# Soft-capped attention and gated convolution on one core: the middle words of the weights copied by GpSimd instead of fetched a second time, and every engine's order written anew

## The chip, the cores and the metric

The program runs on one core of a Trainium2 chip. The metric is the device time of one execution in microseconds (us), taken as the median of repeated runs. The engines are TensorE (PE: matmuls; its weight loads are shown apart as PEld), VectorE (DVE), ScalarE (ACT), GpSimd (POOL) and SyncE (SP, which issues all transfers here).

A measurement of this kernel tells a change from no change at about 0.5%, some 3.5 us.

## The reference

For 8 batches and 12 heads, 448 rows of 64, attention with a soft cap, then a gated feed-forward block on the joined heads (768 wide):

```python
scores = scale * np.matmul(q, k.transpose(0, 1, 3, 2))
scores = cap * np.tanh(scores / cap)
attn = np.exp(scores - max); attn = attn / (sum + 1e-09)
x = matmul(attn, v)                      # heads joined: (8, 448, 768)
gate = 1 / (1 + exp(-sum_k conv_w[k] * x shifted by k))     # 5 taps, per channel
out = (gate * (x @ w_val)) @ w_out
```

The weights `w_val`, `w_out` (768 x 768) and `conv_w` (5 x 768) arrive as 64-bit floats; everything else is float32.

## The kernel before

**Units of work.** Two heads make a pair, so there are 48 pairs, six to a batch; a batch is a block of the feed-forward part.

For a pair: q and k are loaded in 32-wide blocks (`load_blocks`, L335) and turned by DVE (`turn`, L457). PE makes the transposed scores in four chunks of 112 keys for both heads (`scores`, L478, PSUM tile `pss`, two buffers). ACT takes the tanh (L486) and the exp (L490) of each chunk (tile `pt`, 112 x 896).

PE then multiplies the chunk with V (`attnv`, L516, PSUM `psa`) and with ones for the row sums (`sums`, L532, `psz`). For later pairs DVE first adds chunks (`add`, L497 and L500, tile `pa`), so that fewer sums are needed.

DVE turns the sums, adds a guard, takes reciprocals (L538, L545, L546). POOL moves four small pieces of them across partitions (`shift`, L553 and L554, tile `rc`), DVE spreads them (L559) and multiplies (`mul`, L567), which frees `psa`.

From the result `u` follow a rounded copy by ACT (`x_hi`, L572), the rest by DVE (`x_lo`, L392), and five convolution steps (L584 on ACT, L588 on DVE).

From pair 13 on, q and k are also split into a rounded part and a rest (L463 on ACT, L392 on DVE), and a chunk of scores takes three passes in the rounded format, where it took plain float32 before.

For a block: `val` (L619, 3 pairs of column groups, each in four quarters) multiplies the six pairs' `xh`, `xl` with `wv`. The second and fourth quarter need the last three of the six pairs. DVE multiplies with the sigmoid (L594 on ACT; L647), ACT and DVE split the product (L650, L392), `out_part` (also L619) multiplies with `wo`, ACT copies the result out of PSUM (L678) and SP stores it (L682).

**Weights.** They are made in 12 steps of 256 rows by 384 columns. `weight_load` (L424) fetches the 64-bit numbers as pairs of 32-bit words into `w_raw` (one buffer). Of each number the split needs the upper word and a middle one: the upper 16 bits of the lower word next to the lower 16 bits of the upper one.

In the kernel before, `late_load` (L432) fetches the same 64-bit numbers again, shifted by two bytes in SBUF, into `w_late` (one buffer), so that each middle word lies on a word border and is read with a stride of two words.

Then `float64_split` works in three steps: ACT scales the upper word and overwrites it with its sign (L288, L289); DVE makes the high part (L292, L293); DVE masks the middle word and makes the low part (L297 to L299).

The five rows of `conv_w` go the same way, but there the middle words have always been copied by POOL (L320, 60 words of 16 bits).

**What sets the order.** Nothing is scheduled by a tool. The tables PAIRS, BLOCKS and WEIGHTS hold a number for each step, all steps are sorted by it, and each engine gets its instructions in that order. Each engine, SP's queue and POOL's too, works strictly in order. ACT's tanh and exp share a table, the sigmoid has another, and a change between them is an ACT_TABLE_LOAD.

Of the kernel before, what the change touches and what calls it, by code (L numbers as in the profile page):

```python
# [9 lines left out]
I32 = mybir.dt.int32  # L10
U16 = mybir.dt.uint16
# [35 lines left out]
- - -50.2578 -20.0082 -18.6802 - - - - -18.0026 -13.6506 -12.8893 -10.8337 -17.7336 -12.2984 -12.1683 -10.6814  # L47
  -15.7438 -11.0138 -9.0806 -8.4026 - - - -7.8583 -6.6164 -5.2762 -4.8421 -10.8956 -9.6536 -8.227 -6.5272 -6.4187
  -6.2991 -6.0315 -5.2231 -4.7395 -4.0222 -1.5948 -3.3443 -3.1754 -3.0638 -2.2435 -1.4958
-54.6543 -54.6682 -5.7398 -11.3558 -14.9308 - - - - -10.1607 -8.2226 -7.251 -8.8103 -8.766 -7.7723 -6.001 -7.503  # L50
  -7.9851 -7.0271 -5.5705 -7.2509 - - - -4.7942 -4.7791 -4.2203 -3.8644 -6.1487 -5.9805 -5.2522 -5.1652 -4.5697
  -4.2545 -4.0974 -3.8502 -2.9586 -2.9081 -1.1078 -2.6037 -2.0766 -1.4969 -1.2423 -0.7415
-8.5558 -10.828 -3.8585 -8.3819 -8.4517 - - - - -8.1909 -6.7346 -6.2205 -6.6099 -6.9986 -6.3265 -4.9873 -4.745 -6.5847
  -5.8479 -4.4232 -4.2656 - - - -3.5543 -3.3866 -3.1641 -3.0012 -5.1436 -4.2402 -4.2087 -3.8472 -3.7468 -3.4899
  -3.2181 -3.147 -2.6407 -1.157 -0.2141 -2.5015 -2.2091 -2.0732 -0.7817 -0.6342
-4.9902 -5.1452 -3.8143 -4.8984 -4.9319 - - - - -4.8453 -4.8201 -4.7117 -4.5313 -4.7619 -4.5375 -3.7333 -3.8994
  -4.0879 -4.4206 -3.5715 -3.6023 - - - -3.156 -2.3216 -2.1661 -2.1339 -4.0435 -3.5985 -3.5492 -3.322 -2.9828 -2.8443
  -2.611 -2.2872 -1.8844 -0.5716 -0.0119 -1.8513 -1.5372 -1.26 -1.1401 -0.8247
-5.1502 -5.5457 -3.7054 -4.6855 -5.0214 - - - - -4.5836 -4.0485 -4.49 -3.9663 -4.4152 -3.8796 -4.0604 -3.1655 -3.9467
  -3.4539 -3.3349 -3.0695 - - - -2.7667 -2.7181 -2.0325 -1.8895 -3.5521 -3.0355 -3.0189 -2.7694 -2.4562 -2.3389  # L60
  -2.3311 -2.007 -1.5129 -1.4622 -0.436 -1.2333 -0.8715 -0.7915 0.0531 0.3413
-4.7105 -4.9447 -3.6134 -4.1281 -4.1616 - - - - -3.9515 -3.871 -3.5726 -3.6641 -3.8144 -3.7573 -3.4104 -2.6706 -3.7204
  -3.2054 -2.8592 -2.6615 - - - -2.6022 -2.4665 -2.2458 -1.6562 -3.2862 -2.3588 -2.2561 -2.1821 -1.934 -1.9328 -1.728
  -1.6287 -1.5377 -1.4574 -1.2992 -0.1638 0.4232 1.0043 1.0532 1.7255
-3.992 -4.0342 -3.3279 -3.2028 -3.3106 - - - - -2.8324 -2.412 -2.4706 -3.0905 -2.7775 -2.1722 -2.3947 -2.9847 -1.8139
  -1.7614 -1.8089 -1.6615 -1.5463 -1.5365 - -1.8071 -1.3214 -1.0428 -0.828 -1.3963 -1.2032 - - -1.0303 -0.6544 -0.645
  -0.6132 -0.1329 2.0262 2.2951 -0.0875 0.1219 0.4106 1.5565 2.2947
-3.0587 -3.6384 -2.2123 -2.8324 -3.2508 - - - - -2.4022 -1.792 -2.1532 -1.1764 -2.1717 -1.144 -1.7627 -0.9081 -1.0652
  -0.7804 -1.1206 -0.4772 -0.327 -0.2744 - -0.3323 -0.2522 0.0203 0.0481 -0.2338 -0.1371 - - -0.0756 0.0724 0.2788
  0.5812 0.7204 2.5097 3.0808 0.9827 1.2949 2.7809 3.049 3.1704  # L70
# [837 lines left out]
```

## Time and profile before

| | |
|---|---|
| median of 3 runs | 704.95 us (704.92 to 708.12) |
| the profiled execution | 706.22 us, with a span of 704.4 us |
| PE busy | 679.7 us, 96% |
| ACT busy | 575.7 us, 82% |
| DVE busy | 556.7 us, 79% |
| POOL busy | 76.0 us, 11% |
| moved by DMA | 64.14 MB |

The span is what the trace covers, from the first instruction to the last; 1.8 us of the execution lie around it. The shares are means over the whole span, and the engines are not loaded alike in all of it: the weights are made, and the first two blocks' pairs are worked on, in the first 140 us. A count like x1248 is of matmul instructions in the trace, of which a few per cent can be missing.

### The profile page before, as it was taken

To read this page: it belongs to the slowest core of one execution; us is meant where nothing else is said; L and a number is where in the kernel's file an instruction comes from. 1 tells how busy PE (TensorE), PEld (TensorE's weight loads), DVE (VectorE), ACT (ScalarE), POOL (GpSimd) and SP (SyncE) were. 2 spreads that over 40 slices of the span, in tenths; PEclk is the share of its full clock that TensorE was granted. 3 is DMA by queue.
4 is the path that set the end of the run, shared out by engine and by line. 5 is a ranking of instruction groups with operands and counts; after the bars stand their busy time and mean duration, and the time that the engine had idled before them with its cause. 6 is when DMAs were issued, how large, how long until landed. Compare 5 with 4: busy or idle time off the path is not lost.

```text
span 704.4 us, 17118 instructions
## 1 busy us (share of the span) xinstructions
PE 679.7 (96%) x6896; PEld 492.6 (70%) x6896; DVE 556.7 (79%) x972; ACT 575.7 (82%) x738; POOL 76.0 (11%) x260
## 2 busy tenths in 40 slices
PE   5889999999999999999999999999999999999996
PEld 1323665577777787687677787767867878776996
DVE  1699999998897868988889776998897895896530
ACT  5999999988987797887996878878988887986121
POOL 0111100201010002110211100021000100011000
PEclk9999999999999999999999999999999999999999
DMA  6799999954414523243241332434323140211002
GB/s 134 167 190 235 181 213 231 240 122 83 78 32 95 102 41 67 62 92 60 49 80 50 78 72 44 75 77 105 60 53 69 45 111 8 60 38 46 1 3 93
DMA packets 241845, 64.14 MB, mean 91 GB/s; under 512 B 228448, under 2 KB 235616, under 8 KB 241760
## 3 DMA queue, kind: packets, MB, share of 16 engines
q1 hardware_dynamic: 241760, 62.98, 41.6%
q8 instruction: 56, 0.92, 0.6%
q14 instruction: 29, 0.24, 0.1%
HBM read 51.94 MB, written 11.01 MB: 89 GB/s over the span
## 4 chain that ended last, share of the span: by engine, by line
PE 66%; ACT 18%; DVE 6%; issue 3%; SPq 3%; DMA 2%; POOL 1%; ACTq 0%; DVEq 0%; POOLq 0%
PE psf L619 35%; PE psa L516 14%; PE pss L478 12%; ACT pt L486 5%; ACT pt L490 5%; PE pss L619 3%; ACT L490 2%; PE psz L532 2%; SPq L335 2%; ACT L594 1%; ACT g_h L650 1%; DVE pa L500 1%; DVE gate L588 1%; ACT gate L594 1%; POOL rc L553 1%
## 5 line engine op out<-in xcount | busy, mean ns | idle before, releaser
L486 ACT ACTIVATE pt<-pss,rc 112x896 f32<-112x896 f32 x192 | 189.3, 1003 | 42.9 <-PE psa L516 22.1
L490 ACT ACTIVATE pt<-pt,capt 112x896 f32<-112x896 f32 x192 | 194.6, 1041 | 0.9
L619 PE MATMUL psf<-wo,g_h 64*128 64x384 f32 x1248 | 165.0, 338 | 1.3 <-POOL token L627 1.3
L619 PE MATMUL psf<-xh,wv 64*128 64x448 f32 x1104 | 163.0, 369 | 0.2 <-ACT xh L572 0.2
L516 PE MATMUL psa<-pt,vn 112*32 112x448 f32 x1440 | 150.6, 542 | 0.7 <-DVE u L567 0.7
L619 PEld LDWEIGHTS psf<-wo,g_h 64*128 64x128 f32 x1248 | 116.6, 184 | 14.5 <-issue 4.7
L588 DVE SCALAR_TENSOR_TENSOR gate<-u,cw,gate 128x448 f32<-128x448 f32 x192 | 125.4, 664 | 1.4 <-ACT gate L584 0.4
L619 PEld LDWEIGHTS psf<-xh,wv 64*128 64x128 f32 x1104 | 106.5, 184 | 15.3 <-issue 3.8
L619 PE MATMUL psf<-wo,g_l 64*128 64x384 f32 x624 | 108.7, 332 | 0.0
L619 PE MATMUL psf<-xl,wv 64*128 64x448 f32 x552 | 103.8, 362 | 0.0
L500 DVE TENSOR_TENSOR pa<-pt 112x896 f32<-112x896 f32 x84 | 90.2, 1082 | 16.2 <-ACT pt L490 16.0
L516 PEld LDWEIGHTS psa<-pt,vn 112*32 112x32 f32 x1440 | 43.0, 109 | 71.4 <-issue 58.2
L478 PE MATMUL pss<-qt,kt 64*112 64x448 f32 x208 | 50.8, 586 | 13.0 <-DVE guard L401 7.8
L553 POOL COPY rc<-rc 32x7 f32<-32x7 f32 x96 | 32.0, 334 | 281.2 <-DVE rc L546 278.3
L619 PEld LDWEIGHTS psf<-wo,g_l 64*128 64x128 f32 x624 | 62.2, 184 | 0.0
L619 PEld LDWEIGHTS psf<-xl,wv 64*128 64x128 f32 x552 | 54.5, 184 | 3.7 <-DVE xl L392 0.4
L478 PE MATMUL pss<-qh,kh 64*112 64x448 f32 x280 | 54.6, 380 | 0.7 <-ACT pt L486 0.6
L478 PE MATMUL pss<-qh,kl 64*112 64x448 f32 x280 | 52.3, 363 | 0.3 <-DVE kl L392 0.3
L478 PE MATMUL pss<-ql,kh 64*112 64x448 f32 x280 | 52.2, 363 | 0.0
L678 ACT COPY osb<-psf 128x384 f32<-128x384 f32 x52 | 23.0, 481 | 35.0 <-PE psf L619 34.8
L559 DVE STREAM_TRANSPOSE zt<-rc 128x448 f32<-128x448 f32 x48 | 30.8, 641 | 25.8 <-POOL rc L554 25.3
L478 PEld LDWEIGHTS pss<-qt,kt 64*112 64x112 f32 x208 | 17.1, 178 | 36.1 <-ACT pt L486 13.4
(83 smaller groups left out, 812.2 us busy)
## 6 DMA issues: line engine op xcount, KB each, us to landing
vn<-in_v_dram SPq DMA_DIRECT2D x96, 112.0 KB, 2.8
out_dram<-osb SPq DMA_DIRECT2D x56, 192.0 KB, 2.1
kn<-in_k_dram SPq DMA_DIRECT2D x188, 56.0 KB, 2.4
qn<-in_q_dram SPq DMA_DIRECT2D x188, 56.0 KB, 2.5
w_raw<-in_moe_w_val_dram SPq DMA_DIRECT2D x12, 384.0 KB, 4.0
w_late<-in_moe_w_val_dram SPq DMA_DIRECT2D x12, 384.0 KB, 5.2
w_raw<-in_moe_w_out_dram SPq DMA_DIRECT2D x12, 384.0 KB, 3.8
w_late<-in_moe_w_out_dram SPq DMA_DIRECT2D x12, 384.0 KB, 5.5
```

The lines of the kernel that those rows point to most:

```text
L335: nc.sync.dma_start(t[g * BLK:(g + 1) * BLK].rearrange("p (c e) -> p c e", e=BLK), src[b, 2 * hp + j, :, d:d + BLK].rearrange("(c r) e -> ...
L478: nc.tensor.matmul(ps[:CH, j, :S], st[x][r, c], st[y][r], start=(n == 0), stop=(n == len(parts) - 1))
L486: nc.scalar.activation(st["p", i], st.pop(("s", i)), AF.Tanh, scale=rc8[:CH])
L490: nc.scalar.activation(t, t, AF.Exp, scale=capt[:CH])
L500: nc.vector.tensor_tensor(st["a", i], st["p", 2 * i], st["p", 2 * i + 1], op=ALU.add)
L516: nc.tensor.matmul(st["o"][r, :S], vloads[p][:, j, i, d:d + BLK], t[:, j], start=(i == 0), stop=(i == NKT - 1))
L532: nc.tensor.matmul(st["z"][r, :HQ], ones[:CH], t[:, j, q], start=(i == 0), stop=(i == n - 1))
L553: nc.gpsimd.tensor_copy(rc[GROUPS[g], 1], rc[GROUPS[g + 1], 1])
L559: nc.vector.transpose(st["zt"].rearrange("p (c e) -> p c e", e=BLK), rc)
L588: nc.vector.scalar_tensor_tensor(g, u[:, i:i + S], cw[:, hp, i:i + 1], g, ALU.mult, ALU.add)
L619: mm = nc.tensor.matmul(outs[k], left[r], right[r], start=(swap == 0 and first), stop=(swap == 1 and last))
L678: nc.scalar.copy(osb, psums.pop((b, "o", m))[:, :NH])
```

## The change

The second fetch is gone. In its place POOL copies the middle 16-bit words out of `w_raw` into a `w_late` of plain words (1536 of 16 bits for each partition), which DVE then reads without a stride:

```diff
-        def late_load(n):
-            w, c, nh, _ = wsteps[n]
-            late = wsc.tile([P, WC, 4 * NH + 2], U16, name="w_late", bufs=RB)
-            for i in range(WC):
-                r = (c.start + i) * P
-                nc.sync.dma_start(late[:, i, 1:1 + 4 * NH], w[r:r + P, nh * NH:(nh + 1) * NH].bitcast(U16))
-            wlate[n] = shifted(late, NH)
+        def low_words(n):
+            wlate[n] = wsc.tile([P, WC, NH], I32, name="w_late", bufs=RB)
+            nc.gpsimd.tensor_copy(wlate[n].bitcast(U16).rearrange("p i (n k) -> p i n k", k=2), wstate[n].bitcast(U16)[..., 1:3])
...
-            for f, when in zip((weight_load, late_load, weight_first, weight_second, weight_third), row):
+            for f, when in zip((weight_load, low_words, weight_first, weight_second, weight_third), row):
...
-CW_LOAD, CW_AT, W_FREE = -4.6636, -4.1717, 10.9638
+CW_LOAD, CW_AT, W_FREE = 2.1769, 2.7242, 10.5915
```

All three tables have new numbers; of WEIGHTS the first row, for instance:

```diff
--53.6683 -4.7397 -8.071 -6.4898 -4.4784
+0.4627 1.1297 1.297 1.3376 1.4463
```

The line numbers of the changed kernel are smaller by four behind the new function. No instruction is added or removed but the 24 fetches, the 12 copies and 6 ACT_TABLE_LOADs on the path that is taken (45 such loads between exp and sigmoid before, 51 now).

With its new place the copy must read `w_raw` before ACT's sign (L289) overwrites the upper word. It waits for the fetch and for the last read of the `w_late` before it (L299), and the next fetch into `w_raw` waits for the copy.

**DVE, the first weight step.** The rows after the turns of the second pair, before:

```order
L292 TENSOR_SCALAR w_t<-w_t 128x768
L293 TENSOR_TENSOR wv<-w_t,w_raw 128x2x384
L457 STREAM_TRANSPOSE kt<-kn 128x448
L538 STREAM_TRANSPOSE zt<-psz 128x224
L457 STREAM_TRANSPOSE qt<-qn 128x448
L545 TENSOR_SCALAR zt<-zt,guard 128x7
L546 RECIPROCAL rc<-zt 128x14
L559 STREAM_TRANSPOSE zt<-rc 128x448
L567 TENSOR_TENSOR u_63<-psa,zt 128x448
L297 TENSOR_SCALAR w_late<-w_late 128x2x384
L298 TENSOR_SCALAR w_t<-wv 128x768
L299 SCALAR_TENSOR_TENSOR wv<-w_late,w_t 128x2x384
```

The same place now (`u_63` is the result of the first pair):

```order
L292 TENSOR_SCALAR w_t<-w_t 128x768
L293 TENSOR_TENSOR wv<-w_t,w_raw 128x2x384
L297 TENSOR_SCALAR w_late<-w_late 128x768
L298 TENSOR_SCALAR w_t<-wv 128x768
L299 SCALAR_TENSOR_TENSOR wv<-w_late,w_t 128x2x384
L534 STREAM_TRANSPOSE zt<-psz 128x224
L453 STREAM_TRANSPOSE qt<-qn 128x448
L541 TENSOR_SCALAR zt<-zt,guard 128x7
L542 RECIPROCAL rc<-zt 128x14
L453 STREAM_TRANSPOSE kt<-kn 128x448
L555 STREAM_TRANSPOSE zt<-rc 128x448
L563 TENSOR_TENSOR u_63<-psa,zt 128x448
```

The low part of the first step has moved ahead of all of the first pair's division.

**ACT, the second weight step.** The rows from the middle of the third pair on, before (`cw` is the convolution's weights, `w_t` and `w_raw` a weight step, `xh` the rounded copy of a pair's result):

```order
L486 ACTIVATE pt<-pss,rc_110 112x896
L288 ACTIVATE cw_t<-cw_raw 128x30
L289 ACTIVATE cw_raw<-cw_raw 128x30
L572 CAST xh<-u_63 128x448
L490 ACTIVATE pt<-pt,capt 112x896
L584 ACTIVATE gate<-u_63,cw 128x448
L486 ACTIVATE pt<-pss,rc_110 112x896 x2
L490 ACTIVATE pt<-pt,capt 112x896 x2
L288 ACTIVATE w_t<-w_raw 128x768
L289 ACTIVATE w_raw<-w_raw 128x768
```

The same stretch now:

```order
L482 ACTIVATE pt<-pss,rc_110 112x896 x2
L288 ACTIVATE w_t<-w_raw 128x768
L289 ACTIVATE w_raw<-w_raw 128x768
L486 ACTIVATE pt<-pt,capt 112x896
L482 ACTIVATE pt<-pss,rc_110 112x896
L486 ACTIVATE pt<-pt,capt 112x896 x2
L482 ACTIVATE pt<-pss,rc_110 112x896
L288 ACTIVATE cw_t<-cw_raw 128x30
L289 ACTIVATE cw_raw<-cw_raw 128x30
```

The second weight step has moved ahead of the convolution's weights and of the first pair's rounded copy.

**POOL, around the first `val`.** Before, from the end of the sixth pair's division (`rc`) to the seventh's (`token` is a small write that orders two halves of a `val`):

```order
L553 COPY rc_768<-rc_768 32x7
L554 COPY rc_768<-rc_768 32x7
L627 MEMSET token_126 1x1
L553 COPY rc_987<-rc_987 32x7
L554 COPY rc_987<-rc_987 32x7
```

Now, between the same two divisions:

```order
L549 COPY rc_779<-rc_779 32x7
L550 COPY rc_779<-rc_779 32x7
L429 COPY w_late_790<-w_raw_756 128x1536
L623 MEMSET token_126 1x1
L429 COPY w_late_950<-w_raw_888 128x1536
L549 COPY rc_1018<-rc_1018 32x7
L550 COPY rc_1018<-rc_1018 32x7
```

Two of the copies stand in POOL's queue between the two divisions, one ahead of the token and one behind it.

More of the change, by code (lines that the diff above doesn't have):

```diff
@@ L185 @@
[L185 to L190 removed]
+- - 0.559 0.3888 0.6628 - - - - 0.8692 0.6629 1.2962 1.2963 1.1298 0.7229 1.2964 1.2968 1.2965 0.8691 1.2969 1.3452 -
+  - - 1.2967 1.3453 1.5034 1.7231 1.2966 1.2971 1.4464 1.4921 1.6292 1.7235 1.7237 1.9728 1.9729 3.3287 3.591 2.7562
+  2.9091 2.9093 3.0548 3.5031
@@ new lines @@
+-0.3373 -0.131 0.7233 0.1296 0.2961 - - - - 0.4465 0.4466 0.6291 0.568 0.4467 0.492 0.8942 0.6988 0.5681 0.629 0.9029
+  0.8943 - - - 1.0619 1.1767 1.2367 1.5081 0.6989 0.8941 0.985 1.04 1.0618 1.1768 1.3014 1.5077 1.7563 1.9689 1.969
+  1.909 1.9092 2.329 2.5036 3.0097
+-0.8701 -0.7185 0.5079 -0.2768 -0.2764 - - - - -0.097 -0.0969 0.3012 0.1097 -0.0273 0.0399 0.5076 0.3015 0.3679 0.3013
+  0.7243 0.4377 - - - 0.9089 0.997 1.0531 1.4329 0.45 0.7241 0.7561 0.9688 1.5029 1.5032 1.5033 1.5698 1.6311 2.6562
+  3.111 1.7067 2.1467 2.1473 2.1475 2.758
@@ new lines @@
+-1.106 -1.2766 0.433 -0.5622 -0.4511 - - - - -0.399 -0.2072 -0.3391 0.1177 -0.2756 0.1944 0.0532 0.2615 0.0547 0.3629
+  0.1246 0.4328 - - - 0.503 0.5035 0.6312 0.7928 0.3289 0.5204 0.6314 0.633 1.1466 1.1468 1.1472 1.1474 1.1476 2.0439
+  2.2003 1.2164 1.4943 1.7577 1.7579 2.1114
+-1.0029 -0.8822 -0.0574 -0.6712 -0.5669 - - - - -0.5668 -0.4972 -0.2704 -0.3304 -0.4974 -0.4303 0.0096 -0.0576 -0.3631
+  -0.1274 0.1465 0.0767 - - - -0.0139 0.3257 0.3929 0.4296 0.1469 0.2166 0.3927 0.3928 0.6907 0.7578 0.9648 1.1109
+  1.1111 1.2028 1.5126 1.4706 1.7485 1.9949 2.5694 2.697
@@ new lines @@
+-1.0575 -1.4966 -0.6744 -0.8529 -0.9232 - - - - -0.8523 -0.7416 -0.5059 -0.3092 -0.7417 -0.6745 -0.3095 -0.2424
+  -0.6074 -0.5058 -0.1752 -0.1054 - - - -0.2419 -0.1751 0.1108 0.2373 -0.3094 -0.1748 -0.0351 -0.0233 0.1112 0.1113
+  0.1358 0.2029 0.3043 0.4363 0.5802 0.5797 0.9948 1.0634 1.3801 2.9018
+-1.776 -1.7835 -1.1749 -1.1747 -1.7833 - - - - -0.7272 -1.1053 -0.9562 -1.0355 -0.4875 -1.0356 -0.7629 -0.8643 -0.3784
+  -0.8885 -0.1716 -0.2514 -0.005 0.0291 - 0.2396 0.2397 0.2399 0.24 0.2398 0.2403 - - 0.2824 0.3479 0.5696 0.614
+  0.7813 2.7576 2.8321 1.4998 1.5008 1.5487 2.5094 2.8722
@@ new lines @@
+-1.7628 -2.175 -0.3029 -1.4201 -1.5636 - - - - -1.4199 -1.3608 -0.5325 -0.7298 -1.2387 -0.6297 -0.3026 -0.4305 -0.3859
+  -0.2886 -0.2188 -0.3025 -0.2066 -0.1317 - 0.4992 0.4993 0.9017 0.9019 0.4995 0.4996 - - 0.5002 0.5933 1.1009 1.1682
+  1.1686 2.0419 2.0885 2.1287 2.3327 2.4188 2.5757 2.7089
+-2.7626 -2.7273 -0.4996 -2.293 -1.6935 - - - - -0.4999 -1.2185 -0.4991 -1.2186 -0.4997 -0.9236 -0.4927 -0.9907 -0.4994
+  -0.5009 -0.2648 -0.4066 -0.3745 0.1684 - 0.2163 0.2724 0.3285 0.3846 0.1687 0.1881 - - 0.5653 0.5656 0.5657 0.9168
+  1.042 1.3774 2.5913 1.2555 2.5914 2.6951 2.6954 3.0535
@@ new lines @@
+-2.3027 -3.3708 -0.0416 -1.4993 -2.3445 - - - - -1.0299 -1.098 -0.5508 -0.4909 -0.8992 -0.832 -0.4341 -0.2426 -0.5504
+  -0.3168 -0.1677 -0.1622 -0.2427 -0.0417 - 0.3329 0.333 0.3331 0.5756 0.1504 0.3328 - - 0.4634 0.6441 0.6445 0.7535
+  0.8038 1.2379 1.6832 1.2541 1.6829 1.6952 1.9012 2.0534
+-2.8409 -3.0249 -1.2425 -1.4346 -2.4928 - - - - -1.083 -1.3169 -0.8714 -0.9114 -1.0252 -1.0415 -0.5365 -0.5811 -0.534
+  -0.4641 -0.1558 -0.0811 -0.1561 0.3841 - -0.115 -0.0551 0.093 0.0931 0.1133 0.6828 - - 0.7314 0.9011 1.0408 1.1437
+  1.1941 1.3779 1.4061 1.378 1.975 2.0945 2.1479 2.4665
@@ new lines @@
+-2.4274 -2.899 -0.3047 -1.6227 -1.8715 - - - - -1.4876 -0.7623 -1.1559 -1.356 -1.156 -0.6722 -0.9067 -0.9843 0.0409
+  -0.616 -0.4091 -0.85 0.0533 0.0632 0.2756 0.3178 0.406 0.4621 0.5182 0.3778 - - - 0.4226 0.5183 0.5295 0.6325 0.6828
+  0.7335 0.8457 0.9154 0.9304 1.6011 2.4958 3.2074
+-2.8712 -3.1678 -0.1545 -2.0812 -1.7624 - - - - -1.2651 -0.959 -1.6723 -1.409 -0.2322 -0.3171 -1.5565 -1.2501 -0.1546
+  -0.0848 -1.479 -0.9589 0.0477 -0.4811 0.3539 0.2377 0.2976 0.3537 0.4099 0.466 - - - 0.5557 0.5558 0.6014 0.758
+  1.1868 1.4952 1.6562 1.5754 1.6116 1.887 2.2076 2.5684
@@ L237 @@
-2.5692 2.787 3.2505 3.6328 3.7017
-3.9699 4.8797 4.5859 4.8724 5.3787
-5.249 5.6583 5.9805 6.6296 6.6394
-6.7071 6.7617 7.0277 7.1294 7.2018
-7.2689 7.6346 7.8278 8.0635 8.0636
-8.1392 8.1665 8.529 8.8669 8.867
-9.3502 9.706 9.5098 9.869 9.8691
-10.2217 10.2728 10.4887 10.7188 10.7189
+0.4627 1.1297 1.297 1.3376 1.4463
+1.5035 1.973 2.177 2.2368 2.508
+2.5078 3.0533 3.0534 3.0549 3.5205
+3.5027 3.6313 3.7487 4.147 4.2238
+4.2239 4.4944 4.5323 4.9646 4.9647
+4.965 5.2002 5.3042 5.58 5.6217
+5.6218 6.0293 6.0633 6.2703 6.4676
@@ L245 @@
+6.3066 6.8684 6.8685 6.9432 7.0521
+7.0765 7.499 7.6256 7.7353 8.1685
+8.1681 8.4493 8.5092 8.5658 8.6833
+8.9169 9.0194 9.1289 9.1914 9.6444
+9.7536 9.8443 9.945 10.0158 10.0929
 """
-CW_LOAD, CW_AT, W_FREE = -4.6636, -4.1717, 10.9638
+CW_LOAD, CW_AT, W_FREE = 2.1769, 2.7242, 10.5915
 NPAIRED, NPLAIN = 11, 13
```

252 lines of the change are left out of this document (105 added, 147 removed), and 72 rows, old and new, of the table BLOCKS.

## The prediction

> **What bounds the kernel now.** I read the page first, then the table of stretches, then who PE and DVE wait for.
>
> ```profile
> span 704.4 us, 17118 instructions
> PE 679.7 (96%) x6896; PEld 492.6 (70%) x6896; DVE 556.7 (79%) x972; ACT 575.7 (82%) x738; POOL 76.0 (11%) x260
> ```
>
> PE is busy for 679.7 of 704.4 us, so 24.7 us are all that an order can win without taking work from PE. The change takes none: it has the same matmuls. The next table says where the idle time lies (each row: stretch, length, then the busy time of PE, PEld, DVE, ACT and POOL, the clock, the DMA share and GB/s).
>
> ```profile
> core 0: us, PE busy (x) PEld busy (x) DVE busy (x) ACT busy (x) POOL busy (x), PEclk, DMA share, GB/s
> 10.00:30.00 20.00, 17.33 (x130) 5.29 (x128) 7.95 (x15) 19.70 (x23) 0.97 (x5) 1.00 0.84 161
> 30.00:140.00 110.00, 105.73 (x974) 55.07 (x976) 102.70 (x183) 106.84 (x131) 17.45 (x42) 1.00 0.94 212
> 140.00:200.00 60.00, 59.96 (x608) 44.08 (x602) 53.63 (x93) 54.01 (x71) 5.19 (x21) 1.00 0.44 86
> 200.00:400.00 200.00, 198.34 (x2090) 152.36 (x2090) 168.93 (x293) 169.59 (x222) 24.55 (x78) 1.00 0.33 68
> 400.00:600.00 200.00, 198.56 (x2074) 151.91 (x2066) 163.96 (x284) 171.80 (x218) 18.96 (x74) 1.00 0.33 68
> 600.00:698.50 98.50, 97.62 (x1038) 82.81 (x1030) 57.63 (x101) 51.18 (x74) 8.49 (x33) 1.00 0.13 37
> 698.50:704.40 5.90, 0.00 (x0) 0.00 (x0) 0.00 (x0) 0.86 (x2) 0.00 (x0) 0.86 0.22 72
> ...
> ```
>
> Three parts are to be told apart. From 140 to 698.5 us PE alone is the bound: it idles for 558.5 - 554.5 = 4.0 us, while ACT and DVE are busy for four fifths of it (446.6 and 444.2 us). At the end 5.9 us go to the last copy and store. From 10 to 140 us three engines are full at once: PE idles for 130 - 123.1 = 6.9 us, ACT is busy for 126.5 of 130, DVE from 30 us on for 102.7 of 110, and the DMA engines for 0.94 of the time. All of the weights' work lies in this part, so it decides.
>
> ```profile
> PE pss L478 <- DVE guard L401: 7.8, 1, 7.8
> PE pss L478 <- ACT pt L486: 4.0, 8, 1.3
> ...
> ```
>
> Of PE's waits (total, times, longest) 7.8 us are the start, before the first scores, and what stands ahead of them on SP and DVE stays as it was. The next is for ACT's tanh, which frees the scores' PSUM tile. For a transfer PE does not wait. DVE's waits from 30 to 140 us begin so:
>
> ```profile
> DVE zt L559 <- POOL rc L554: 2.3, 6, 0.5
> ...
> DVE w_late L297 <- DMA w_late<-in_moe_w_out_dram: 0.5, 1, 0.5
> ```
>
> **The fetch that goes.**
>
> ```profile
> w_late<-in_moe_w_val_dram SPq DMA_DIRECT2D x12, 384.0 KB, 5.2
> w_late<-in_moe_w_out_dram SPq DMA_DIRECT2D x12, 384.0 KB, 5.5
> ```
>
> 24 transfers of 384 KB are 9.4 MB, out of the DMA's busiest time. What waited for them, though, is the 0.5 us above, on DVE. I take 0, with -0.5 as the other end: the load on the DMA engines falls, but nobody stands behind them.
>
> **ACT's and PE's order in the first part.** As ACT is full there, a PE step that needs an ACT result comes as late as the ACT work ahead of that result, and what matters is that sum against the PE work ahead of the step. I counted both in the two orders, up to the first `val` quarter of a block that needs the block's sixth `xh`. Prices:
>
> ```profile
> L486 ACT ACTIVATE pt<-pss,rc 112x896 f32<-112x896 f32 x192 | 189.3, 1003 | 42.9 <-PE psa L516 22.1
> L490 ACT ACTIVATE pt<-pt,capt 112x896 f32<-112x896 f32 x192 | 194.6, 1041 | 0.9
> L289 ACT ACTIVATE w_raw<-w_raw 128x768 f32<-128x768 f32 x12 | 11.2, 929 | 0.4
> L288 ACT ACTIVATE w_t<-w_raw 128x768 f32<-128x768 f32 x12 | 11.0, 914 | 0.0
> L584 ACT ACTIVATE gate<-u,cw 128x448 f32<-128x448 f32 x11 | 7.2, 658 | 0.0
> L594 ACT ACTIVATE gate<-gate 128x448 f32<-128x448 f32 x48 | 26.2, 573 | 2.3 <-DVE gate L588 2.0
> ```
>
> In block 0, ACT now has one tanh, one exp and one weight step more ahead of it, and one convolution step less: 1.00 + 1.04 + 1.84 - 0.66 = +3.2 us, while PE has only one chunk of scores more to do meanwhile. In block 1 it has two tanh less and one sigmoid more, -2.0 + 0.6 = -1.4 us, and PE one chunk of split scores less, three passes at 0.2 us (the pitch of L478 further below): -0.8 us net. So PE starts its first block later and has caught up by the second. Where PE falls furthest behind decides, and by the same count of the order before that was at block 1's place: I take -0.3 us, with -0.8 and +2.4 as ends.
>
> **PE's changes of format.** Counted in the order, PE goes from the rounded format to plain float32 and back 54 times before and 57 times now. One such excursion:
>
> ```profile
> 208.19 0.34 PE L619 MATMUL psf<-wo,g_l 64*128 64x384 f32 x2
> 208.46 0.96 PE L516 MATMUL psa<-pt,vn 112*32 112x448 f32 x8
> ...
> 211.98 0.46 PE L478 MATMUL pss<-qh,kh 64*112 64x448 f32 x2
> 212.28 0.36 PE L478 MATMUL pss<-ql,kh 64*112 64x448 f32 x2
> 212.48 0.37 PE L478 MATMUL pss<-qh,kl 64*112 64x448 f32 x2
> ```
>
> The way out costs about 0.1 us (0.27 where a pitch of 0.17 was due), the way back 0.1 us (0.30 in place of the 0.20 between the next two). Three more are +0.6 us.
>
> **ACT's table loads** rise from 45 to 51, at the price of this row:
>
> ```profile
> L490 ACT ACT_TABLE_LOAD x22 | 28.2, 1283 | 0.3
> ```
>
> That is 7.7 us of ACT. Up to block 1's place both orders have six changes of table, so the new ones lie behind it, where ACT waits for PE (of its 42.9 us ahead of tanh, 22.1 are for a matmul): 0. Without that cover it would be up to 7.7 us.
>
> **The copy on POOL.** Its form is in the trace once, with 60 words of 16 bits, as `cw_m`; around it stand a small copy that nothing disturbed, and a longer POOL instruction beside an idle DVE:
>
> ```profile
> L320 POOL COPY cw_m<-cw_raw 128x60 uint16<-128x60 uint16 x1 | 0.2, 234 | 1.5 <-DMA cw_raw<-in_moe_conv_w_dram 1.5
> 39.25 0.18 POOL L554 COPY rc<-rc 32x7 f32<-32x7 f32 x1
> 642.24 0.51 POOL L657 TENSOR_SCALAR g_h<-g_h 128x384 fp32r<-128x384 f32 x1
> ```
>
> From 7 to 60 elements the time rises by 0.05 us, from 7 to 384 by 0.33: about 0.9 ns for one. 1536 make 0.2 + 1.4 = 1.6 us, twelve times 19 us on an engine that has 17.45 of 110 us busy. The best case that the Trainium skill names (GPSIMD Engine Reference, section 3.1), 1.8 cycles for an element at 1.2 GHz, would make it an estimated 2.3 us; the rows here are faster.
>
> POOL's own time costs nothing. What it does to DVE may:
>
> ```profile
> 39.28 0.97 DVE L293 TENSOR_TENSOR wv<-w_t,w_raw 128x768 fp32r<-128x768 f32 x1
> 39.47 0.83 POOL L553 COPY rc<-rc 32x7 f32<-32x7 f32 x1
> ...
> 340.17 2.39 DVE L500 TENSOR_TENSOR pa<-pt 112x896 f32<-112x896 f32 x2
> 340.86 0.76 POOL L657 TENSOR_SCALAR g_h<-g_h 128x384 fp32r<-128x384 f32 x1
> 341.58 1.34 POOL L657 TENSOR_SCALAR g_l<-g_l 128x384 fp32r<-128x384 f32 x1
> 342.59 1.28 DVE L497 TENSOR_TENSOR pa<-pa,pa 112x896 f32<-112x896 f32 x1
> L500 DVE TENSOR_TENSOR pa<-pt 112x896 f32<-112x896 f32 x84 | 90.2, 1082 | 16.2 <-ACT pt L490 16.0
> ```
>
> A copy of 0.18 us took 0.83 because it came during a DVE instruction with two SBUF inputs, and ended with it. The other way round, two adds of 1.08 us took 2.39, 0.23 too long, and the next 0.2 too long, when POOL came between. So each holds the other up.
>
> The Trainium skill (SBUF — State Buffer, section "SBUF: two separate sides") has a rule for it: the two engines share one pair of ports as an exclusive lock, held for a whole instruction, and only DVE instructions in a two-port mode or with two SBUF inputs take part. By that rule alone a copy would stop such a DVE instruction for all of its 1.6 us; these rows agree in kind, at 0.2 us for an instruction of under half a microsecond.
>
> Two of the twelve copies come before 27 us, where DVE is mostly idle. For each of the other ten I bound DVE's loss by 0 (DVE is in its turns or in an instruction that reads PSUM) and 1.6 us (stopped for a whole copy). I take half, 0.8 us, since in the rows above POOL cost DVE 0.2 of its 0.4: 8 us. Against it stand 110 - 102.7 = 7.3 us of DVE idle time, of which some 5 can be used, and the low part of the first weight step, which now runs before the first pair's division:
>
> ```profile
> 27.53 0.57 DVE L297 TENSOR_SCALAR w_late<-w_late 128x768 int32<-128x768 int32 x1
> ...
> 28.60 0.96 DVE L299 SCALAR_TENSOR_TENSOR wv<-w_late,w_t 128x768 fp32r<-128x768 int32 x1
> ```
>
> From 27.53 to 29.56 that is 2.0 us out of the full part. 8 - 5 - 2 = +1.0 us, with 0 and 16 - 7 = +9 as ends. Behind a copy in POOL's queue stand the `rc` pieces for which DVE waits, and the `token` for which PE waits; behind ACT's sign (L289), which waits for the copy, stands all of ACT's work. The order puts the copies between two divisions, and ACT has the scaling (L288) to do ahead of the sign, so I take 0; if every copy began only as ACT came to its weight step, it would be 12 x (1.6 - 0.9) = 8 us.
>
> **The sum.** -0.3 + 0.6 + 0 + 1.0 = +1.3 us on a span of 704.4: 705.7, or 707.5 us with the 1.8 us around it. The profiled execution, 706.22 us, lies 1.3 us above the median of the runs, 704.95; from the median the forecast is **706.3 us**, no change that can be measured (0.5% is 3.5 us: 701.4 to 708.5).
>
> **Rivals.**
>
> *Slower: DVE becomes the bound of the first part.* If the copies stop DVE for their whole length, it loses 16 us there and can absorb 7: +9, and with the +0.3 of the other terms 714 us. It decides from (3.2 + 7) / 10 = 1.0 us of loss for one copy. For it: the 0.83 us row, and a DVE that already leaves only 7%. Against it: about a third of DVE's instructions there are turns or read PSUM. Signs that wait for their copies, above, would add to it. The time would be that of the lock in the Trainium skill (SBUF — State Buffer, "SBUF: two separate sides"), held at its fullest; the rows here show the lock, and none shows how long a copy of this size holds it. Chance 0.33.
>
> *Faster: the new order closes gaps.* The 6.9 us of PE idle time from 10 to 140 us and the 4.0 us behind it are what it could win; half of it is 5.5 us, which gives 699.5 us. For it: the DMA engines go from 0.94 to about two thirds, so loads come early, and all steps were free to move. Against it: ACT is busy for 126.5 of 130 us, and the same ACT work stands ahead of block 1. Chance 0.20.
>
> *That the second fetch stays, or the copies wait for it,* can't be: the order has no such row.
>
> **How the numbers follow.** No change has 0.47, slower 0.33, faster 0.20, each with a spread of some 3 us around its time. The range is 700 to 714 us: it leaves out a tenth at either end, and its upper end is the full stop of DVE. Within the no-change case alone it is 702 to 708.5.
>
> **What would show it.** In the profile after, POOL should have twelve copies of about 1.6 us (a mean up to 2.5, as they wait for DVE), the DMA share from 30 to 140 us about 0.65, DVE's busy time there some 5 us higher, and PE's idle time from 10 to 140 us within 3 us of 6.9. The first block's `val` should start some 2 us later than before, and the second block's where it was. The forecast is wrong if PE idles for 10 us or more there behind DVE, or for under 3; if the copies take over 3 us; or if PE's idle time behind 140 us leaves 4.0 by more than 2 us.

## The result and the profile after

| | before | after |
|---|---|---|
| median, first comparison (4 runs each) | 704.93 us | 713.38 us (712.28 to 714.16) |
| ratio | | 1.0108, 95% interval 1.0076 to 1.0140 |
| repeated beside other kernels (11 runs before, 5 after) | 707.06 us | 712.53 us, ratio 1.0080 (1.0067 to 1.0094) |

The change made the kernel slower by 0.8 to 1.1%. The range on record, 700 to 714 us, holds the time, though only just. The likeliest case, no change, was wrong, and so were two steps of its sum. Everything below is given as a ratio to the kernel before, run on the same chip in the same group; 1% is 7.1 us.

The page of the kernel after: span, then busy time and share of each engine.

```profile
span 712.0 us, 17107 instructions
PE 680.6 (96%) x6896; PEld 491.8 (69%) x6896; DVE 565.5 (79%) x972; ACT 583.7 (82%) x744; POOL 103.7 (15%) x272
```

PE's own work is the same (679.7 us before). DVE executes the same 972 instructions, but they take 8.8 us longer. The stretches of the kernel after (stretch, length, busy time of PE, PEld, DVE, ACT, POOL, clock, DMA share, GB/s):

```profile
30.00:140.00 110.00, 100.99 (x915) 53.82 (x909) 103.50 (x174) 102.15 (x127) 30.29 (x48) 0.98 0.63 131
...
10.00:140.00 130.00, 119.16 (x1063) 60.31 (x1061) 112.72 (x192) 121.92 (x148) 35.07 (x57) 0.99 0.66 131
140.00:698.00 558.00, 549.64 (x5728) 421.36 (x5726) 450.94 (x773) 457.46 (x589) 68.14 (x208) 1.00 0.30 63
```

The DMA share from 30 to 140 us fell from 0.94 to 0.63, as announced. But PE idles from 10 to 140 us for 10.8 us, where it was 6.9, and from 140 to 698 us for 8.4 us, where it was 4.0. So about 4 us were lost in each of two parts, and they have to be explained apart. PE's waits behind 140 us in the kernel after (total, times, longest):

```profile
PE psf L615 <- POOL token L623: 4.3, 4, 1.5
PE pss L474 <- ACT pt L482: 1.5, 2, 0.8
PE pss L474 <- DVE ql L392: 1.1, 2, 0.9
PE psa L512 <- DVE u L563: 0.9, 2, 0.6
PE psz L528 <- DVE pa L493: 0.7, 2, 0.4
```

These are 8.5 us. The same list of the kernel before adds up to 3.8 us, and begins so:

```profile
PE psf L619 <- POOL token L627: 1.3, 2, 1.0
PE psa L516 <- DVE u L567: 0.7, 2, 0.4
```

No copy begins behind 140 us, so this loss looks like one of the order. The copies themselves, in the kernel after (durations in ns: shortest, median, longest; then the first and the last start):

```profile
L429 POOL COPY w_late<-w_raw x12: 1464/1466/2118, 10.9 to 139.5; 128x1536 uint16<-128x1536 uint16 x12
```

What one of them does is seen at 115 us, in the timeline of the kernel after (start, duration, then in brackets the idle time before and who ended it):

```profile
114.98 0.62 DVE L563 TENSOR_TENSOR u<-psa,zt 128x448 f32<-128x448 f32 x1
115.38 1.46 POOL L429 COPY w_late<-w_raw 128x1536 uint16<-128x1536 uint16 x1 [3.90 <-DMA w_raw<-in_moe_w_out_dram]
115.51 1.81 DVE L392 TENSOR_TENSOR g_l<-gate,g_h 128x448 fp32r<-128x448 f32 x1
...
117.24 1.14 DVE L643 TENSOR_TENSOR gate<-psf,gate 128x448 f32<-128x448 f32 x2
117.89 0.56 ACT L646 CAST g_h<-gate 128x448 fp32r<-128x448 f32 x1 [3.71 <-DVE gate L643]
...
119.76 0.58 DVE L392 TENSOR_TENSOR g_l<-gate,g_h 128x448 fp32r<-128x448 f32 x1
...
124.00 1.01 PE L474 MATMUL pss<-qt,kt 64*112 64x448 f32 x4 [1.87 <-ACT pt L482]
```

The subtraction `g_l` takes 0.58 us at 119.76 and 1.81 us at 115.51, where the copy came with it. It ends at 117.32, about half a us behind the copy's end at 116.84, as if most of its work had begun only then. The product `gate` behind it on DVE is late by that, and ACT ends a wait of 3.7 us only then. PE still has work at that time; it pays at 124.00, where it waits 1.87 us for ACT. In the same order without copies (a kernel of the next section) ACT's wait is 1.14 us and PE's 0.42:

```profile
111.78 0.57 ACT L648 CAST g_h<-gate 128x448 fp32r<-128x448 f32 x1 [1.14 <-DVE gate L645]
...
117.87 1.01 PE L476 MATMUL pss<-qt,kt 64*112 64x448 f32 x4 [0.42 <-ACT pt L484]
```

Read in this way, ten copies lengthened DVE's instructions by 0 to 1.3 us each, 7.3 us in all.

### The profile page after: what moved, and what is told of

Read it like the earlier page. It is cut to its first block, busy times and chain, and to the rows that moved or that the text cites. A ratio compares the mean times of both kernels' runs of the same rounds, so it can differ in the third digit from the quotient of the medians.

```text
span 712.0 us, 17107 instructions
## 1 busy us (share of the span) xinstructions
PE 680.6 (96%) x6896; PEld 491.8 (69%) x6896; DVE 565.5 (79%) x972; ACT 583.7 (82%) x744; POOL 103.7 (15%) x272
## 4 chain that ended last, share of the span: by engine, by line
PE 58%; ACT 12%; DVE 11%; issue 2%; POOL 1%; DMA 1%; SPq 1%; ACTq 0%; DVEq 0%; POOLq 0%
PE psf L615 32%; PE psa L512 12%; PE pss L474 9%; ACT pt L486 4%; ACT pt L482 3%; PE pss L615 3%; ACT L486 2%; PE psz L528 2%; DVE gate L584 2%; DVE pa L496 2%; ACT g_h L646 1%; DVE pa L493 1%; DVE gate L643 1%; POOL rc L549 1%; DVE zt L555 1%
## 5 line engine op out<-in xcount | busy, mean ns | idle before, releaser
L496 DVE TENSOR_TENSOR pa<-pt 112x896 f32<-112x896 f32 x84 | 92.0, 1103 | 22.9 <-ACT pt L486 22.5
L549 POOL COPY rc<-rc 32x7 f32<-32x7 f32 x96 | 36.2, 378 | 283.7 <-DVE rc L542 281.2
L474 PE MATMUL pss<-qt,kt 64*112 64x448 f32 x208 | 52.3, 597 | 13.0 <-DVE guard L401 7.9
L646 ACT CAST g_h<-gate 128x448 fp32r<-128x448 f32 x48 | 26.4, 561 | 32.6 <-DVE gate L643 32.6
L643 DVE TENSOR_TENSOR gate<-psf,gate 128x448 f32<-128x448 f32 x46 | 27.3, 613 | 26.8 <-PE psf L615 26.8
```

The lines of the kernel that those rows point to most:

```text
L474: nc.tensor.matmul(ps[:CH, j, :S], st[x][r, c], st[y][r], start=(n == 0), stop=(n == len(parts) - 1))
L496: nc.vector.tensor_tensor(st["a", i], st["p", 2 * i], st["p", 2 * i + 1], op=ALU.add)
L549: nc.gpsimd.tensor_copy(rc[GROUPS[g], 1], rc[GROUPS[g + 1], 1])
L643: nc.vector.tensor_tensor(g, psums.pop((b, d))[:, :S], g, op=ALU.mult)
L646: nc.scalar.copy(gated["h"][:, d, TL:], gates[b * NPAIR + d])
```

## The experiments

**Theory A**: the copies stop DVE, and in a part where DVE has no time to spare the end is late by about as much. **Theory B**: the order written anew is what costs. A third question came up on the way: what the second fetch was worth.

| kernel | median | ratio to before | interval |
|---|---|---|---|
| old order, no fetch, no copy | 705.05 us | 0.9973 | 0.9960 to 0.9986 |
| old order, copies | 712.44 us | 1.0080 | 1.0066 to 1.0094 |
| old order, copies in four pieces | 707.96 us | 1.0015 | 1.0001 to 1.0030 |
| old order, SBUF-to-SBUF transfers | 734.77 us | 1.0394 | 1.0367 to 1.0420 |
| new order, no fetch, no copy | 707.16 us | 1.0005 | 0.9996 to 1.0014 |
| new order, copies (the change, repeated) | 712.53 us | 1.0080 | 1.0067 to 1.0094 |
| new order, copies in four pieces | 709.83 us | 1.0045 | 1.0031 to 1.0059 |
| new order, copies in eight pieces | 711.51 us | 1.0062 | 1.0044 to 1.0081 |
| new order, each copy twice | 722.36 us | 1.0215 | 1.0202 to 1.0229 |
| new order, spare copies later | 710.68 us | 1.0050 | 1.0036 to 1.0064 |
| new order, second fetch | 722.65 us | 1.0225 | 1.0206 to 1.0244 |
| new order, second fetch issued later | 717.74 us | 1.0146 | 1.0124 to 1.0168 |

### The change taken apart

**The order alone**: the new tables, with `late_load` in place of the copy, issued together with the first fetch.

```diff
-            for f, when in zip((weight_load, low_words, weight_first, weight_second, weight_third), row):
-                at(when, f, n)
+            for f, when in zip((weight_load, late_load, weight_first, weight_second, weight_third), row):
+                at(row[0] if f is late_load else when, f, n)
```

> The new order alone: every step stands where the changed kernel has it, but the middle parts are fetched a second time, as before, and GpSimd copies nothing. Theory A (the copies' hold on VectorE costs the first part its 5 to 6 us, the order only some 3 us behind it, less 2 us at the end): 706 to 708 us, PE idle from 10 to 140 us near 7 us. Theory B (the new order itself makes the kernel slower): 711 to 714 us, PE idle from 10 to 140 us still near 11 us. In both, PE's waits for the token on POOL stay as in the changed kernel if they belong to the order.

Measured 1.0225, outside of both. PE's waits in this kernel:

```profile
PE pss L478 <- DVE guard L401: 7.8, 1, 7.8
PE psa L516 <- DMA vn<-in_v_dram: 6.8, 4, 2.4
PE psf L619 <- POOL token L627: 4.3, 4, 1.5
PE psf L516 <- DMA vn<-in_v_dram: 3.4, 2, 2.2
```

And those of SP's queue from 10 to 145 us (L432 is the second fetch):

```profile
SPq L432 <- DVE wv L299: 10.9, 5, 3.8
SPq L432 <- DVE wo L299: 8.1, 4, 3.1
```

PE now waits 10.2 us for `vn`, for which it never waited in the kernel before: the second fetch waits 19 us in SP's queue for its buffer, with the loads of q, k and v behind it. So this run can't judge between A and B; it shows that the new order does not go with a second fetch at this place. The waits for the token are those of the kernel after (4.3 us), so they do belong to the order.

**The copy alone**: the old tables and `low_words` as in the change, at a place between the landing and the scaling.

```diff
+                if f is low_words:
+                    when = row[2] - 0.0001 if n == 0 else (max(row[0], done) + row[2]) / 2
```

> The copy alone: the order of before, the second fetch gone, and each GpSimd copy placed midway between the landing of its weights (and the end of the weight step ahead) and its scaling on ScalarE. Theory A: ten copies stop VectorE for about 0.7 us each, of which the 7 us of idle time take a part; 708 to 712 us, and PE's idle time behind 140 us stays near 4 us. Theory B: 704 to 706 us.

Measured 1.0080, 5.7 us, as A has it (712.44 us is 0.4 above A's range, but the kernel before is 1.8 us slower in this group than the 704.95 us that the range was reckoned from). Behind 140 us PE idles for 4.4 us, near the 4.0 of the kernel before, as A said too.

**The new order without fetch and copy**; `lates[0]` is one tile, set to 1.0 once, so this kernel leaves out the middle words of the weights:

```diff
-            nc.gpsimd.tensor_copy(wlate[n].bitcast(U16).rearrange("p i (n k) -> p i n k", k=2), wstate[n].bitcast(U16)[..., 1:3])
+            wlate[n] = lates[0]
```

> The changed kernel without its copies and without a second fetch: the low parts are computed from one constant tile, so the low halves of the weights are wrong, and VectorE, ScalarE and TensorE have the same instructions in the same order as in the changed kernel. Theory A: 706 to 708 us, with VectorE's busy time from 30 to 140 us some 6 us lower. Theory B: 712 to 714 us. Beside the run with the order alone it shows what the second fetch costs in this order: both within 1 us if it costs nothing.

Measured 1.0005: A's value. Its page and its two stretches:

```profile
PE 678.5 (96%) x6896; PEld 490.7 (69%) x6896; DVE 558.2 (79%) x972; ACT 583.3 (82%) x744; POOL 83.7 (12%) x261
```

```profile
10.00:140.00 130.00, 123.31 (x1120) 63.14 (x1118) 111.45 (x201) 127.52 (x156) 15.61 (x45) 0.99 0.72 137
140.00:698.00 558.00, 549.55 (x5742) 423.54 (x5741) 444.93 (x764) 452.99 (x585) 67.02 (x208) 1.00 0.30 63
```

Without the copies PE idles 6.7 us in the first part, as before the change. Behind 140 us it still idles 8.5 us (8.4 with the copies), so that loss is the order's and not the copies'. DVE's busy time over the whole span is 7.3 us lower than with the copies, as read off one by one above. From 30 to 140 us it is only 1.5 us lower (102.05 against 103.50), where 6 were expected; that sign missed.

**The kernel before without its second fetch**, the same edit in the old order, and **the change again**, beside it:

> The kernel before in its old order, without the second fetch and without any copy: the low parts come from one constant tile, so the low halves of the weights are wrong. If the fetch cost nothing in the old order: the time of before within 1 us. If the DMA's load of 0.94 did hold something up: 1 to 5 us faster. Against the kernel without copies in the new order (equal to before) it says which of the two orders is the better one once neither has a fetch or a copy: the same if the orders are worth the same, 2 us or more faster if the new order loses what I read in its trace behind 140 us.

> The changed kernel again, unaltered, beside the others of this group. Its ratio to the kernel before should come out near the first one, 1.0108; what the kernel without copies (ratio 1.0005) lies below it is the price of the copies in the new order.

Measured 0.9973 and 1.0080. With these the corners can be subtracted. They come from two groups on two chips, each set against its own runs of the kernel before; by the intervals in the table each difference holds to 1 to 1.5 us:

- The fetch that goes: 0.9973 - 1 = -0.27%, -1.9 us.
- The order, with neither fetch nor copy: 1.0005 - 0.9973 = +0.32%, +2.3 us.
- The copies in the new order: 1.0080 - 1.0005 = +0.75%, +5.3 us; in the old order 1.0080 - 0.9973 = +1.07%, +7.6 us.

The timelines say where the copies' price is paid. PE's first `val` matmul of block 1 and its last matmul, in the new order without copies and then with them:

```profile
158.02 0.67 PE L617 MATMUL psf<-xh,wv 64*128 64x448 f32 x4
...
700.95 0.34 PE L617 MATMUL psf<-wo,g_l 64*128 64x384 f32 x2
```

```profile
162.76 0.68 PE L615 MATMUL psf<-xh,wv 64*128 64x448 f32 x4
...
705.97 0.34 PE L615 MATMUL psf<-wo,g_l 64*128 64x384 f32 x2
```

And the old order without copies and with them:

```profile
159.07 0.58 PE L617 MATMUL psf<-xh,wv 64*128 64x448 f32 x4
...
696.91 0.34 PE L617 MATMUL psf<-wo,g_l 64*128 64x384 f32 x2
```

```profile
166.30 0.58 PE L615 MATMUL psf<-xh,wv 64*128 64x448 f32 x4
...
704.08 0.34 PE L615 MATMUL psf<-wo,g_l 64*128 64x384 f32 x2
```

In the new order PE is 4.7 us late at block 1 and 5.0 us at the end, in the old one 7.2 us at both places. All of the price is paid before block 1, and PE wins back nothing of it later, where it idles for only 4 to 9 of 558 us. The spans of the first pair differ by less, 707.4 and 710.8 us: from the start of the last matmul to the end it took 6.4 us in one execution and 4.8 in the other.

The clock is a rival that the rows can answer. In the old order the granted clock is 1.00 from 30 to 140 us with copies and without, and there they cost most. In the new order it is 0.98 in both traces. Of the five runs of the change repeated, the one with a mean clock of 1.0 took 711.96 us and the four at 0.995 to 0.997 took 712.25 to 713.43, while nine of the eleven without copies had 0.999 or 1.0; so an estimated half a us of the 5.3 may be the clock's.

### Is it DVE that the copies stop?

**Each copy twice**, one behind the other:

```diff
             nc.gpsimd.tensor_copy(wlate[n].bitcast(U16).rearrange("p i (n k) -> p i n k", k=2), wstate[n].bitcast(U16)[..., 1:3])
+            nc.gpsimd.tensor_copy(wlate[n].bitcast(U16).rearrange("p i (n k) -> p i n k", k=2), wstate[n].bitcast(U16)[..., 1:3])
```

> The changed kernel with each GpSimd copy done twice, one behind the other. Theory A: VectorE has no idle time left to absorb a second copy, so ten more copies at 0.7 to 1.5 us each add 7 to 15 us: 720 to 728 us. Theory B: under 2 us more, 713 to 715 us.

Measured 1.0215, 9.5 us above the single copy: A. Its page:

```profile
PE 682.5 (95%) x6896; PEld 491.4 (68%) x6896; DVE 573.7 (80%) x972; ACT 583.5 (81%) x744; POOL 127.0 (18%) x284
```

The second copies lengthened DVE's work by 8.2 us (573.7 against 565.5). ACT's signs wait for a copy for 6.4 us there, 0.3 with the single copy, so not all of the 9.5 us need be DVE's.

**Four pieces**, of one row block and half its columns each:

```diff
-            nc.gpsimd.tensor_copy(wlate[n].bitcast(U16).rearrange("p i (n k) -> p i n k", k=2), wstate[n].bitcast(U16)[..., 1:3])
+            o, i = wlate[n].bitcast(U16).rearrange("p i (n k) -> p i n k", k=2), wstate[n].bitcast(U16)[..., 1:3]
+            for j in range(WC):
+                for h in range(2):
+                    r = slice(h * NPH * P // 2, (h + 1) * NPH * P // 2)
+                    nc.gpsimd.tensor_copy(o[:, j, r], i[:, j, r])
```

> The changed kernel with each copy cut into four pieces of 384 elements (0.4 us each by the measured 1.47 us for 1536). If VectorE loses time because one GpSimd instruction holds the port until it ends, a piece can stop it for 0.4 us at most and the two take turns: 709 to 712 us, with VectorE's instructions stretched by under 0.5 us each. If the loss goes with the words copied and not with the length of one instruction: 713 to 714 us, as the changed kernel.

Measured 1.0045, 709.83 us, the first of the two, with the copies' price cut from 0.75 to 0.40%. The mechanism shows in one small instruction, the mask of the convolution's weights (L298 on 30 words), in the kernels without copies, with whole ones, with four pieces and with eight:

```profile
35.46 0.18 DVE L298 TENSOR_SCALAR cw_t<-cw 128x30 int32<-128x30 int32 x1
```

```profile
35.80 1.47 POOL L429 COPY w_late<-w_raw 128x1536 uint16<-128x1536 uint16 x1 [3.41 <-DMA w_raw<-in_moe_w_val_dram]
...
35.89 1.42 DVE L298 TENSOR_SCALAR cw_t<-cw 128x30 int32<-128x30 int32 x1
```

```profile
35.92 0.96 POOL L433 COPY w_late<-w_raw 128x384 uint16<-128x384 uint16 x2 [0.69 <-DMA w_raw<-in_moe_w_val_dram]
...
36.01 0.46 DVE L298 TENSOR_SCALAR cw_t<-cw 128x30 int32<-128x30 int32 x1
```

```profile
34.43 2.57 POOL L433 COPY w_late<-w_raw 128x192 uint16<-128x192 uint16 x8 [2.17 <-DMA w_raw<-in_moe_w_val_dram]
...
35.83 0.33 DVE L298 TENSOR_SCALAR cw_t<-cw 128x30 int32<-128x30 int32 x1
```

0.18 us of work take 1.42, 0.46 or 0.33 us, following the length of one GpSimd instruction (medians of 1.47, 0.51 and 0.35). The Trainium skill (SBUF — State Buffer, section "SBUF: two separate sides") describes a pair of ports that GpSimd and a DVE instruction take as an exclusive lock for a whole instruction, and these rows agree with it: DVE's instruction ends just behind the end of one on POOL (37.31 and 37.27 us with whole copies).

**Eight pieces** (`range(4)` and quarters of the columns in the code above):

> The changed kernel with each copy in eight pieces of 192 elements. By the lock held for one instruction, a piece stops VectorE for some 0.3 us at most: ratio between 1.001 and 1.004 (four pieces gave 1.0045, no copies 1.0005), if GpSimd's longer total time (some 33 us of copies instead of 18) makes no sign wait. If the loss only follows the number of collisions: 1.0045 or more.

Measured 1.0062, no better than four; by the medians it is worse, but the intervals overlap. By its size this is the second branch, but the condition of the first did not hold either: cut this small, the twelve copies take POOL longer in all (96 x 0.352 = 33.8 us by the median of a piece), and signs do wait. ACT's waits from 10 to 140 us:

```profile
ACT pt L486 <- PE pss L478: 3.8, 1, 3.8
ACT w_raw L289 <- POOL w_late L433: 3.1, 4, 0.9
```

With four pieces the signs wait 0.7 us in all. DVE also waits 5.9 us for a load of q with eight. Whether either of the two ate up the gain is not shown; cutting finer than four brought nothing more.

**Spare copies later**: the new order without copies, and twelve that nobody needs between 204 and 584 us (1408 elements each).

```diff
+        for n in range(12):
+            at(15.5 + 2.5 * n, spare_copy, n % 4)
```

> The kernel without copies (new order, low halves wrong), with twelve copies that nobody needs put between about 240 and 640 us, one every 35 us or so, each of 1408 elements in the same form. VectorE is busy there for 84% and TensorE is the bound. If a copy costs only where VectorE has no time to spare: within 1.5 us of the kernel without copies, so a ratio of 0.999 to 1.003. If a copy costs its 0.5 us wherever it stands: 712 to 714 us, ratio near 1.009.

Measured 1.0050, between the two expectations. The page and the two stretches:

```profile
PE 678.7 (96%) x6896; PEld 490.5 (69%) x6896; DVE 566.5 (80%) x972; ACT 583.1 (82%) x744; POOL 103.6 (15%) x273
```

```profile
10.00:140.00 130.00, 122.41 (x1114) 61.88 (x1112) 112.11 (x200) 127.27 (x155) 16.80 (x45) 1.00 0.72 137
140.00:698.00 558.00, 549.17 (x5732) 423.24 (x5730) 452.57 (x765) 453.24 (x586) 85.64 (x219) 1.00 0.30 62
```

Here too DVE's work grows by 8.3 us (566.5 against 558.2). In the stretch with the copies PE's busy time is only 0.4 us smaller (549.17 against 549.55), but a fixed stretch does not hold the same work in both. So the two matmuls from above are the better measure, here in the kernel with the spare copies:

```profile
158.72 0.68 PE L622 MATMUL psf<-xh,wv 64*128 64x448 f32 x4
...
702.87 0.34 PE L622 MATMUL psf<-wo,g_l 64*128 64x384 f32 x2
```

At block 1 PE is 0.7 us later than without copies (158.02), at the end 1.9 (700.95). The first 0.7 us stand ahead of every spare copy; they may come from the edit's other side (the constant tile lies elsewhere and is read in another way), which was not tested. The copies cost PE the other 1.2 us, a seventh of what DVE lost, where in the first part 5.3 of 7.3 us were lost. So where PE alone is the bound most of it is hidden, and not all. The timed difference, 0.45% or 3.2 us, is larger than these 1.9. Most of the rest is that the profiled execution without copies, 709.25 us, lay 2.1 us above its median, and the one with the spare copies 0.6; the clock of the former fell to 0.91 from 30 to 50 us, where the other's stayed at 1.00.

### What could take the copy's place

**The second fetch issued later**, behind the end of the weight step that frees its buffer:

```diff
-                at(row[0] if f is late_load else when, f, n)
+                at(max(row[0], done + 0.0001) if f is late_load else when, f, n)
```

> The new order with the second fetch (no copy), but each second fetch issued only behind the end of the weight step ahead, which frees its buffer, and no longer together with the first fetch. If the 15 us of the run with the order alone come from SP's queue, where the loads of q, k and v stand behind a fetch that waits for its buffer: 707 to 711 us (ratio 1.001 to 1.006), and PE waits for vn no longer. If they come from the bytes themselves (DMA share): still 718 us or more.

Measured 1.0146, a third of the way back and next to the second expectation. Over the first 160 us the queue's waits of these two kinds at L432 fell only from 23.0 to 19.9 us, so SP comes to the fetch early all the same, and the waits for `vn` to 6.9 us. That the place in the queue is a part of the price is shown; how much the bytes themselves cost in this order is not settled.

**A transfer from SBUF to SBUF**, in the old order:

```diff
-            nc.gpsimd.tensor_copy(wlate[n].bitcast(U16).rearrange("p i (n k) -> p i n k", k=2), wstate[n].bitcast(U16)[..., 1:3])
+            nc.gpsimd.dma_start(late[:, :, 1:1 + 4 * NH], wstate[n].bitcast(U16).rearrange("p i n k -> p i (n k)"))
```

> A version meant to beat both: the old order, the weights fetched once, and the middle parts made by a transfer from SBUF to SBUF (the raw words again, shifted by 16 bits) issued from GpSimd's queue as soon as the buffer is free, in place of the copy. The old order with neither fetch nor copy has ratio 0.9973. If the transfers land before ScalarE comes to its sign: 0.997 to 1.000, and VectorE's busy time as in that kernel (556 us). If the signs wait for the landing, 1 to 2 us for each of twelve: 1.015 to 1.03.

Measured 1.0394, by the second branch and beyond it. Its transfers (KB and median us from issue to landing) and ACT's and SP's waits from 10 to 140 us:

```profile
w_late<-w_raw POOLq DMA_DIRECT2D x12, 768.0 KB, 5.3
```

```profile
ACT w_raw L289 <- DMA w_late<-w_raw: 19.8, 8, 4.3
...
SPq L424 <- DMA w_late<-w_raw: 32.3, 9, 5.1
```

Eight signs wait 19.8 us in all, and the next fetch into the one `w_raw` waits too, with the loads behind it.

**Four pieces in the old order**, the two edits above together:

> The old order with the copy in four pieces (as the copy alone, 1.0080, but each copy cut into four of 384 elements). Without fetch and copy the old order has 0.9973, so whole copies cost 1.07% there. If the pieces' gain belongs to the port and not to the order, they save here what they saved in the new order, 0.35% or somewhat more: ratio 1.002 to 1.005. If what they gained in the new order was a matter of that order's places: 1.007 to 1.009.

Measured 1.0015, a little better than expected: the pieces save 0.65% here. It is the best version with one fetch, clearly faster than the change, and no faster than the kernel before. With nothing in the fetch's place the better of the two orders has 0.9973, and the cheapest copies tried cost 0.40 to 0.42%.

## Why the prediction was right or wrong

**The copy's length and its hold on DVE: right.** 1.6 us was forecast, 1.47 measured. (One row behind that was misread: at 642.24 DVE was not idle but in a turn, L559, from 642.18 to 642.83; turns ran undisturbed beside the copies as well.) The Trainium skill's best case (GPSIMD Engine Reference, section 3.1), which made an estimated 2.3 us, did not hold here. For DVE's loss I took 0.8 us for each of ten, 8 us; the trace shows 7.3.

**"8 - 5 - 2 = +1.0": the step that failed.** It let DVE's idle time absorb 5 us and the moved low part 2 us. The copies cost 5.3 us of the 7.3 in the new order, so some 2 us were absorbed there; they cost 7.6 in the old one, and the second copies 9.5. DVE's idle time is a poor store to draw on: a late DVE result makes ACT and then PE late, as from 115 to 124 us, and DVE's next idle time is then spent waiting for them. DVE's busy time in the stretch rose only from 102.7 to 103.5 us for that reason, so this sign, which I had put at +5, was badly chosen; over the whole span it rose by 8.8.

**The order, "-0.3 + 0.6": wrong by its reach.** The count stopped at block 1. Up to there it was near the truth: without copies PE idles 6.7 us in the first part, against 6.9, and 7.3 in the old order without the fetch. Behind 140 us I looked at the table loads and format changes alone. There the waits rise from 3.8 to 8.5 us, above all those for POOL's token, from 1.3 to 4.3. PE's busy time (678.5 against 678.2 us in the two kernels without fetch and copy) leaves little for the format changes. ACT's part, 1.5 in place of 0.6 us at the scores, may be the table loads; that was not tested. In the time the order costs 2.3 us. The two profiled executions differ by more, 4.4 us (709.25 and 704.85), as the first lay 2.1 us above its median; what the order wins ahead of block 1 was not taken apart.

**The fetch, 0 with -0.5 as an end: too little.** It was worth 1.9 us. Without it block 1's `val` starts at 159.1 in place of 160.4 us; no wait on DMA had announced that.

**Rivals.** The slower one had the time (714) and the mechanism, with two errors that cancelled: a loss of 1.6 us for each copy, twice the true one, and 7 us absorbed, where 2 us or nothing was. Its point of decision, 1.0 us for a copy, was therefore wrong: 0.7 was enough. The faster one's gaps did not close. That the range holds the time is in part luck: its upper end, 714, is the middle of the slower rival, at a chance of 0.33, so about a sixth was left out above it and not a tenth.

**Signs.** The first `val` came 2 us later (73.3 for 71.1 us), as said; block 1's, at 164.3 for 160.4, did not come back to its place. The first part's idle time left 6.9 by 3.9 us, the one behind by 4.4, and either alone contradicts the forecast.

The sum, for the repeated run: -1.9 + 2.3 + 5.3 = +5.7 us, where the forecast had 0 + 0.3 + 1.0 = +1.3.

## What to carry to other kernels

Where three engines are full at once, time taken from one of them is not absorbed by the idle share that its row shows; reckon most or all of it as lost, and count only on a stretch with a single, other bound to hide most of it. A GpSimd instruction on SBUF can stop a DVE instruction for nearly its own length (1.2 of 1.47 us here), so cut long ones, and stop when their total time begins to make somebody wait. And an order is priced to the end of the program, and with the work it was made for: the same tables cost 2.3 us without the second fetch, and with it, issued together with the first, the kernel ran 15.9 us slower than before.

## What the runs showed of the hardware

- A POOL copy of 16-bit words at a stride takes 1.47 us for 1536 elements of a partition, 0.51 for 384 and 0.35 for 192: 0.83 ns for one more, and 0.2 us for the instruction.
- A DVE instruction with one SBUF input (L298, int32) was stopped by the copy like those with two. A transposition (0.65 us at 72.94) and a product that reads PSUM (0.62 us at 73.69) ran beside the copy at 72.97 at their usual length:

```profile
72.94 0.65 DVE L555 STREAM_TRANSPOSE zt<-rc 128x448 f32<-128x448 f32 x1 [0.54 <-POOL rc L550]
73.69 0.62 DVE L563 TENSOR_TENSOR u<-psf,zt 128x448 f32<-128x448 f32 x1
```

- 768 KB from SBUF to SBUF take 5.3 us to land, beside 3.5 to 4.0 us for the 384 KB of a weight load in the same kernel.
- The granted clock was 0.98 from 30 to 140 us in the kernel after, in its repeat and in the new order without copies, 1.00 there in the kernel before, with the copies in pieces and with the spare copies; what sets it was not tested.
